# Softmax row sums by query halves, one reciprocal from PSUM, and a spread that is issued a pair later

## The chip, the cores and the metric

One core of a Trainium2 chip runs the kernel. The metric is the device time in microseconds of one execution. TensorE multiplies matrices, VectorE and ScalarE work on tiles (ScalarE has tanh, exp and silu), GpSimd here casts small tiles and issues transfers, SP issues the other transfers. Each engine takes its instructions in the order of the program; a waiting instruction holds up all that stand behind it on its engine.

## What is computed

```python
scores = scale * np.matmul(q, k.transpose(0, 1, 3, 2))      # 2 x 12 heads, 448 tokens, 64 wide
scores = cap * np.tanh(scores / cap)
attn = np.exp(scores - scores.max(-1)) / sum                 # softmax
x = attn @ v                                                 # 896 tokens x 768
h = x @ w_in;  g = h * sigmoid(1.702 * h);  x = g @ w_out     # 768 -> 2048 -> 768
xn = x / rms(x) * rms_g
out = (silu(xn @ w_gate) * (xn @ w_val)) @ w_out2            # 768 -> 1536 -> 768
```

All in float32. Matmuls whose operands are split into a high and a low part (float32r) take three products; the products with the exponentials as moving operand are plain float32, which TensorE runs as two passes, so one `matmul` call is two MATMUL instructions in the trace.

## The kernel before, in words

The program is written out in order by hand (a manual schedule), so the order of the calls is the order on every engine. It has two stages.

**Attention** (`attention`, L176 to L483) goes over 12 pairs of heads (NPR = 12). For pair p: `turn` transposes q and k (seven transposes), `split_kq` splits them on VectorE and casts a small block on GpSimd (L268); `scores(p, c)` for c = 0, 1, 2 makes the transposed scores of 128 keys by 448 queries for both heads, `scores_last` those of the last 64 keys of both heads in one tile; `exps` runs tanh and exp on ScalarE; the results are `pt[p, c]`, with keys on partitions. No maximum is subtracted. `outputs(p)` multiplies them with v into one PSUM bank, 64 partitions per head, and copies the bank to `zt[p]` (L331, for the last pair on ScalarE, L333). `sums(p)` multiplies them with ones to get the row sums.

The row sums have to reach all 64 partitions of a head, as reciprocals. For the first nine pairs `sums` makes two partial sums per head on 32 columns of the array each (L347: four products side by side, two rounds), copies the bank to SBUF (L352), and four small transfers on GpSimd's queue (L357) lay the 2 x 2 rows out over 128 partitions by 7. `recips(p)` adds the halves (L377), takes the reciprocal of 128 x 7 (L378) and sends it to DRAM (L380, the tile recs); `spread(p)` reads it back, each row to 64 partitions (L387, the tile r). For the last three pairs `sums` makes the sums on all 64 partitions of a head at once (L363, L368) and takes a reciprocal of 128 x 448 from PSUM (L373). `normal(p)` is `norm_mul` (L390, z times r), `norm_hi` (L395 or, for the last two pairs, L397 on ScalarE) and `norm_lo` (L401): it writes the high and low part of x.

The loop at L438 runs p = 0 to 12. In iteration p, in this order: exps(p, 0) and (p, 1); scores(p, 2); scores(p+1, 0); one decode operation; exps(p, 2); scores_last(p); turn and split of pair p+2; exps(p, 3); recips and spread of p-3; outputs(p-1); scores(p+1, 1); normal(p-4), and in the last two iterations normal(p-2) too; more decode operations; sums(p-1); loads. PSUM holds two tiles of scores, one of the turn (`ps_t`) and two banks (`ps_v`) that scores_last, outputs and sums share.

**Decode.** The weights arrive as 64-bit words; `square`, `sign`, `mask` and `high_part` on ScalarE and `mid`, `top`, `low` and `low_part` on VectorE turn a unit of them into a high and a low float32r part. `low(w)` also issues the load of unit w+3 on SP's queue (L151). The first four units are decoded within attention from a list of 30 operations (`early`, L417), of which each iteration from p = 3 on takes some in order.

**Feed-forward** (`rest`, L485 on) is three products per block (L541 to L543) and the last projection (L744). Its first six columns are units 0 to 2 on the first 384 tokens, then on the other 512; between the first and the second column `normal` of the last pair is issued (L605).

Of the kernel before, what the change touches and what calls it, by code (L numbers as in the profile page):

```python
# [18 lines left out]
def attn_moe_kernel(  # L19
# [38 lines left out]
    ones = keep.tile([128, 128], F32R, name="ones")  # L58
    gcol = keep.tile([128, KD], F32, name="gcol")
# [116 lines left out]
    def attention():  # L176
        with ExitStack() as actx:
# [19 lines left out]
            def constants():  # L197
# [5 lines left out]
                for e in range(2):  # L203
                    nc.gpsimd.memset(blk[half[e], half[e]], 1.0)
                    nc.gpsimd.memset(blk[half[e], half[1 - e]], 0.0)

# [127 lines left out]

            def sums(p):

                ps = ps_v.tile([128, 512], F32, tag="v", name="v")
                if p < NPR - 3:
                    for n in range(2):
                        for e in range(2):  # L340
                            for j in range(2):
                                if n and j:
                                    w, t = blk[:, 64 * e:64 * e + 32], pt[p, NC]
                                else:
                                    w, t = f(ones)[:, 0:32], pt[p, j + 2 * n][:, e]
                                r0 = 64 * e + 32 * j
                                nc.tensor.matmul(  # L347
                                    out=ps[r0:r0 + 32, 0:S], lhsT=w, rhs=t,
                                    start=(n == 0), stop=(n == 1), skip_group_check=True,
                                )  # L350
                    sc = zrp.tile([128, S], F32, tag="sc", name="sc", bufs=2)
                    nc.vector.tensor_copy(sc, ps[:, 0:S])  # L352
                    nr[p] = zrp.tile([128, 2, S // 64], F32, tag="rs", name="rs", bufs=3)
                    for e in range(2):
                        for j in range(2):
                            r0 = 64 * e + 32 * j
                            nc.gpsimd.dma_start(  # L357
                                out=nr[p][half[e], j], in_=sc[r0:r0 + 1, :].rearrange("o (a n) -> o a n", a=64)
                            )
                else:  # L360
                    for c in range(NC):
                        for e in range(2):
                            nc.tensor.matmul(  # L363
                                out=ps[half[e], 0:S], lhsT=f(ones)[:, half[e]], rhs=pt[p, c][:, e],
                                start=(c == 0), stop=False, skip_group_check=True,
                            )
                    for e in range(2):
                        nc.tensor.matmul(  # L368
                            out=ps[half[e], 0:S], lhsT=blk[:, half[e]], rhs=pt[p, NC],
                            start=False, stop=True, skip_group_check=True,  # L370
                        )
                    nr[p] = zrp.tile([128, S], F32, tag="r", name="r", bufs=3)
                    nc.vector.reciprocal(out=nr[p], in_=ps[:, 0:S])  # L373

            def recips(p):
                rs = nr[p]
                nc.vector.tensor_tensor(out=rs[:, 0], in0=rs[:, 0], in1=rs[:, 1], op=ALU.add)  # L377
                nc.vector.reciprocal(out=rs[:, 0], in_=rs[:, 0])  # L378
                nr[p] = dram.tile([2, S], F32, tag="recs", name="recs")
                nc.gpsimd.dma_start(  # L380
# [43 lines left out]
            def decode(n):  # L424
                for _ in range(min(n, len(early))):
                    run(*early.popleft())
# [423 lines left out]
```

## Time and profile before

| what | value |
|---|---|
| median of 3 runs (lowest to highest) | 639.77 us (637.91 to 642.45) |
| the profiled execution | 638.68 us |
| its span, first to last instruction | 636.9 us |
| TensorE busy | 612.9 us, 96% |
| VectorE busy | 437.8 us, 69% |
| ScalarE busy | 399.8 us, 63% |
| GpSimd busy | 82.8 us, 13% |
| mean granted TensorE clock | 0.994 |

Times in rows are microseconds from the start of the span. PE is TensorE, PEld its weight loads, DVE VectorE, ACT ScalarE, POOL GpSimd. A busy TensorE is one with a matmul in flight, not one at its peak. A row of the timeline gives start, duration, engine, line, operation, output and inputs with their shapes, and in brackets the idle time before it and what ended that. The granted clock is a share of 2.4 GHz.

### The profile page before, as it was taken

How to read it: one execution, taken by the hardware profiler on the slowest of the kernel's cores; microseconds unless marked ns; L12 is line 12 of the kernel's file. 1: busy time of each engine (PE TensorE's matmuls, PEld its weight loads, DVE VectorE, ACT ScalarE, POOL GpSimd, SP SyncE). 2: the span in 40 equal slices, each digit the busy share in tenths (PEclk: the TensorE clock that was granted, in tenths of full speed). 3: DMA queues.
4: the chain of work that ended last, by engine and by line, in shares of the span. 5: the costliest groups of instructions: out<-in, count | busy, mean ns of one | idle time of the engine just before them, and what ended most of it. 6: DMA issues, size and time to landing. Idle time of an engine off the chain costs nothing.

```text
span 636.9 us, 8389 instructions
## 1 busy us (share of the span) xinstructions
PE 612.9 (96%) x3251; PEld 511.6 (80%) x3251; DVE 437.8 (69%) x553; ACT 399.8 (63%) x533; POOL 82.8 (13%) x125
## 2 busy tenths in 40 slices
PE   7999878789999999999999999999999999999997
PEld 4544434348888998999888888999998899999997
DVE  2446765596768544566778889999378887588842
ACT  5999848719777564677867666668345676355500
POOL 2233432200000000000002220310012200023100
PEclk9999997999999999999999999999999999999999
DMA  5674523222334343133333423334323234143012
GB/s 132 151 187 118 132 52 97 78 65 81 118 103 146 104 145 99 51 100 125 125 99 100 143 64 102 139 100 150 98 69 131 99 100 150 58 134 106 0 57 117
DMA packets 86230, 67.22 MB, mean 106 GB/s; under 512 B 40228, under 2 KB 83510, under 8 KB 86192
## 3 DMA queue, kind: packets, MB, share of 16 engines
q1 hardware_dynamic: 80448, 64.27, 33.2%
q0 software_dynamic: 4784, 2.20, 1.4%
q8 instruction: 25, 0.41, 0.3%
q10 hardware_dynamic: 960, 0.23, 0.2%
q14 instruction: 13, 0.11, 0.1%
HBM read 63.80 MB, written 2.78 MB: 105 GB/s over the span
## 4 chain that ended last, share of the span: by engine, by line
PE 82%; DMA 8%; DVE 4%; ACT 3%; SPq 2%; issue 1%; POOL 0%; ACTq 0%; DVEq 0%; POOLq 0%
PE b L543 21%; PE b L542 21%; PE b L541 21%; PE b L744 14%; DMA r<-recs 4%; DMA recs<-rs 2%; PE v L320 2%; ACT tt L310 1%; PE s L288 1%; DMA kq<-in_q 1%; DVE r L373 1%; SPq L218 1%; DMA kq<-in_k 1%; DMA raw<-in_moe_w_in 1%; PE v L298 1%
## 5 line engine op out<-in xcount | busy, mean ns | idle before, releaser
L541 PE MATMUL b<-x,ring 128*128 128x512 f32 (+1 forms) x480 | 173.9, 362 | 2.0 <-DVE r L373 2.0
L543 PE MATMUL b<-x,ring 128*128 128x512 f32 (+1 forms) x480 | 174.2, 363 | 0.0
L542 PE MATMUL b<-x,ring 128*128 128x512 f32 (+1 forms) x480 | 174.0, 363 | 0.0
L541 PEld LDWEIGHTS b<-x,ring 128*128 128x128 f32 x480 | 90.1, 188 | 12.7 <-DVE r L373 2.3
L542 PEld LDWEIGHTS b<-x,ring 128*128 128x128 f32 x480 | 90.1, 188 | 9.8
L543 PEld LDWEIGHTS b<-x,ring 128*128 128x128 f32 x480 | 90.1, 188 | 9.4
L136 DVE SCALAR_TENSOR_TENSOR dec<-raw,dec 128x768 uint32<-128x768 uint32 x68 | 69.7, 1025 | 26.7 <-ACT dec L132 25.3
L744 PE MATMUL b<-ring,uA 128*128 128x384 f32 x504 | 87.8, 334 | 0.0
L744 PEld LDWEIGHTS b<-ring,uA 128*128 128x128 f32 x504 | 87.4, 188 | 0.0
L157 ACT ACTIVATE ring<-dec 128x768 fp32r<-128x768 f32 x68 | 56.7, 834 | 30.7 <-DVE dec L148 23.0
L142 DVE SCALAR_TENSOR_TENSOR dec<-raw,dec 128x768 uint32<-128x768 uint32 x68 | 73.2, 1076 | 1.1
L543 PE MATMUL b<-g,ring 128*128 128x384 f32 (+1 forms) x192 | 70.0, 365 | 0.0
L542 PE MATMUL b<-g,ring 128*128 128x384 f32 (+1 forms) x192 | 69.9, 364 | 0.0
L541 PE MATMUL b<-g,ring 128*128 128x384 f32 (+1 forms) x192 | 69.6, 362 | 0.0
L162 DVE TENSOR_TENSOR ring<-dec,ring 128x768 fp32r<-128x768 f32 x68 | 66.8, 984 | 3.6 <-ACT ring L157 3.6
L148 DVE SCALAR_TENSOR_TENSOR dec<-raw,dec 128x768 uint32<-128x768 uint32 x68 | 64.9, 955 | 1.4
L128 ACT ACTIVATE dec<-dec,edge 128x768 f32<-128x768 f32 x68 | 63.3, 932 | 0.9
L124 ACT ACTIVATE dec<-raw 128x768 f32<-128x768 f32 x68 | 61.0, 896 | 1.3 <-DVE ring L162 0.5
L132 ACT ACTIVATE dec<-dec 128x768 f32<-128x768 f32 x68 | 57.3, 843 | 1.5
L712 POOL TENSOR_TENSOR a<-a,gg 128x512 f32<-128x512 f32 (+1 forms) x18 | 29.7, 1648 | 188.6 <-DVE gg L705 188.6
L715 ACT ACTIVATE uA<-a 128x512 fp32r<-128x512 f32 (+1 forms) x24 | 13.9, 578 | 46.4 <-POOL a L712 34.5
L636 POOL TENSOR_TENSOR sqs<-sqs,sq 128x384 f32<-128x384 f32 (+1 forms) x10 | 11.7, 1169 | 236.0 <-ACT sq L632 236.0
(99 smaller groups left out, 706.9 us busy)
## 6 DMA issues: line engine op xcount, KB each, us to landing
raw<-in_moe_w_out SPq DMA_DIRECT2D x20, 768.0 KB, 4.2
raw<-in_moe_w_in SPq DMA_DIRECT2D x16, 768.0 KB, 4.6
raw<-in_moe_w_gate SPq DMA_DIRECT2D x12, 768.0 KB, 4.2
raw<-in_moe_w_val SPq DMA_DIRECT2D x12, 768.0 KB, 4.2
raw<-in_moe_w_out SPq DMA_DIRECT2D x8, 512.0 KB, 3.9
out<-oacc SPq DMA_DIRECT2D x6, 384.0 KB, 2.3
raw<-in_moe_w_out SPq DMA_DIRECT2D x8, 256.0 KB, 3.3
r<-recs POOLq DMA_DIRECT2D x9, 224.0 KB, 8.2
```

What stands on the lines that cost most here:

```text
L124: nc.scalar.activation(out=f(d), in_=f(r[:, :, 1]), func=AF.Square, scale=2.0 ** 15)
L128: nc.scalar.activation(out=f(d), in_=f(d), func=AF.Sign, bias=edge)
L132: nc.scalar.activation(out=f(d), in_=f(d), func=AF.Relu, scale=2.0 - 2.0 ** -23)
L136: nc.vector.scalar_tensor_tensor(out=d, in0=hi, scalar=3, in1=d, op0=ALU.logical_shift_left, op1=ALU.bitwise_and)
L142: nc.vector.scalar_tensor_tensor(out=d, in0=hi, scalar=0xC0000000, in1=d, op0=ALU.bitwise_and, op1=ALU.bitwise_or)
L148: nc.vector.scalar_tensor_tensor(out=d, in0=lo, scalar=29, in1=d, op0=ALU.logical_shift_right, op1=ALU.bitwise_or)
L157: nc.scalar.activation(out=t[:, 0], in_=f(dec_t[w][0]), func=AF.Copy)
L162: nc.vector.tensor_tensor(out=t[:, 1], in0=f(d), in1=f(t[:, 0]), op=ALU.subtract)
L541: nc.tensor.matmul(out=wide(o, b), lhsT=w0, rhs=x0, start=first, stop=False)
L542: nc.tensor.matmul(out=wide(o, b), lhsT=w0, rhs=x1, start=False, stop=False)
L543: nc.tensor.matmul(out=wide(o, b), lhsT=w1, rhs=x0, start=False, stop=last)
L744: nc.tensor.matmul(out=os_[t][n][:, 0:HW], lhsT=uA[xi][:, i, tok], rhs=w[:, wi, n * HW:(n + 1) * HW], start=(i == 0 and xi == 0 and wi == ...
```

## The change

- `sums` is one form for all pairs: for each head and each half of the 448 queries (224 columns), a product with ones (or, for the last keys, with `blk`) on 32 columns of the array, over all four blocks of keys. The result is 4 groups of 32 equal rows by 224 columns. One reciprocal of 128 x 224 reads it from PSUM.
- For the first nine pairs `keep_recips` sends one row of each group to DRAM right after `sums`; `spread` reads it back in the next iteration, ahead of that iteration's `sums`. The four small transfers, the copy, the add and `recips` are gone.
- For the last three pairs `spread_product` spreads the rows with four products with a selecting matrix `sel` (made by GpSimd at the start) into PSUM: pairs 9 and 10 in one tile of `ps_t` in iterations 11 and 12, pair 11 behind the first column of feed-forward. `norm_mul` reads them there.
- `norm_mul` writes into z in place of r; `norm_hi` of pair 10 is on VectorE.
- The decode list becomes a plan by iteration; what it has for p = 12 comes after the loop.

```diff
             def sums(p):
                 ps = ps_v.tile([128, 512], F32, tag="v", name="v")
...
+                for c in range(NC + 1):
                     for e in range(2):
                         for j in range(2):
+                            if c == NC:
+                                w, t = blk[:, 64 * e:64 * e + 32], pt[p, NC]
+                            else:
+                                w, t = f(ones)[:, 0:32], pt[p, c][:, e]
                             r0 = 64 * e + 32 * j
+                            nc.tensor.matmul(
+                                out=ps[r0:r0 + 32, 0:SH], lhsT=w, rhs=t[:, j * SH:(j + 1) * SH],
+                                start=(c == 0), stop=(c == NC), skip_group_check=True,
                             )
+                nr[p] = zrp.tile([128, SH], F32, tag="rs", name="rs", bufs=4)
+                nc.vector.reciprocal(out=nr[p], in_=ps[:, 0:SH])
+
+            def keep_recips(p):
+                rs = nr[p]
+                nr[p] = dram.tile([4, SH], F32, tag="recs", name="recs", bufs=3)
+                nc.gpsimd.dma_start(out=nr[p], in_=rs[0:128:32])
+
+            def spread(p):
+                d = nr[p].rearrange("(e j) n -> e (j n)", j=2)
+                nr[p] = zrp.tile([128, S], F32, tag="r", name="r", bufs=3)
+                nc.gpsimd.dma_start(out=nr[p], in_=d.unsqueeze(1).to_broadcast([2, 64, S]))
+
+            def spread_product(p, ps):
+                for j in range(2):
                     for e in range(2):
                         nc.tensor.matmul(
+                            out=ps[half[e], j * SH:(j + 1) * SH], lhsT=sel[:, 2 * e + j], rhs=nr[p],
+                            start=True, stop=True, skip_group_check=True,
                         )
+                nr[p] = ps[:, 0:S]
...
-            early = deque(
...
+            plan = {
+                3: [(square, 0), (sign, 0)], 4: [(mask, 0)], 5: [(square, 1), (mid, 0)],
+                6: [(sign, 1), (mask, 1), (top, 0), (low, 0)], 7: [(high_part, 0), (mid, 1)],
+                8: [(square, 2), (top, 1), (low_part, 0)], 9: [(sign, 2), (low, 1)],
+                10: [(mask, 2), (high_part, 1), (mid, 2)],
+                11: [(square, 3), (sign, 3), (top, 2), (low, 2), (low_part, 1)],
+                12: [(mask, 3), (high_part, 2), (low_part, 2), (mid, 3), (top, 3), (low, 3)],
+            }
...
-                if 3 <= p < NPR:
-                    recips(p - 3)
-                    spread(p - 3)
                 if p >= 1:
                     outputs(p - 1)
...
                 if p >= 4:
                     normal(p - 4)
+                if p == NPR - 1:
+                    late = ps_t.tile([128, 2, 512], F32, tag="t", name="late")
                 if p >= NPR - 1:
+                    spread_product(p - 2, late[:, p - NPR + 1])
                     normal(p - 2)
-                if 2 < p < NPR:
-                    decode((2, 3, 4)[max(0, p - NPR + 3)])
+                if p < NPR:
+                    decode(p)
+                if p >= 2 and p - 2 < NPR - 3:
+                    spread(p - 2)
                 if p >= 1:
                     sums(p - 1)
+                    if p - 1 < NPR - 3:
+                        keep_recips(p - 1)
...
+                        later(lambda: spread_product(q3, bank()))
                         later(*[lambda fn=fn: fn(q3) for fn in (norm_mul, norm_hi, norm_lo)])
```

## Rows read from the trace of the kernel before

**Rows 1.** The page's chain that ended last, by line

```profile
PE b L543 21%; PE b L542 21%; PE b L541 21%; PE b L744 14%; DMA r<-recs 4%; DMA recs<-rs 2%; PE v L320 2%; ACT tt L310 1%; PE s L288 1%; DMA kq<-in_q 1%; DVE r L373 1%; SPq L218 1%; DMA kq<-in_k 1%; DMA raw<-in_moe_w_in 1%; PE v L298 1%
```

**Rows 2.** Table of stretches: busy time (instructions) of each engine, granted clock

```profile
core 0: us, PE busy (x) PEld busy (x) DVE busy (x) ACT busy (x) POOL busy (x), PEclk, DMA share, GB/s
...
85.00:95.00 10.00, 6.71 (x47) 2.70 (x45) 6.61 (x12) 2.41 (x4) 4.22 (x9) 1.00 0.11 26
95.00:105.00 10.00, 6.70 (x28) 4.45 (x30) 3.31 (x5) 8.84 (x11) 2.70 (x5) 0.66 0.54 141
...
160.00:636.90 476.90, 473.54 (x2422) 434.21 (x2420) 346.25 (x421) 282.55 (x394) 41.35 (x28) 1.00 0.32 104
```

**Rows 3.** Timeline of VectorE, ScalarE and TensorE around 95 us

```profile
93.41 0.63 DVE L390 TENSOR_TENSOR r<-z,r 128x448 f32<-128x448 f32 x1 [2.30 <-DMA r<-recs]
...
96.03 0.84 ACT L157 ACTIVATE ring<-dec 128x768 fp32r<-128x768 f32 x1 [8.55 <-DVE dec L148]
...
97.82 1.49 PE L288 MATMUL s<-x 64*128 64x448 f32 x6 [4.96 <-ACT tt L310]
```

**Rows 4.** Waits in 14 to 143 us: total, times, longest

```profile
POOL r L387 <- DMA recs<-rs: 33.5, 9, 5.0
```

**Rows 5.** Timeline of VectorE: z copies of pairs 2 and 10

```profile
42.81 0.62 DVE L331 COPY z<-v 128x448 f32<-128x448 f32 x1 [0.60 <-PE v L325]
...
125.74 0.62 DVE L331 COPY z<-v 128x448 f32<-128x448 f32 x1 [3.56 <-PE v L325]
```

**Rows 6.** Timeline of TensorE: sums of pair 1 and iteration 3

```profile
34.87 1.31 PE L347 MATMUL v<-tt,ones 128*32 128x448 f32 x9
...
36.51 1.50 PE L288 MATMUL s<-x 64*128 64x448 f32 x12
...
39.51 2.48 PE L320 MATMUL v<-tt,vn 128*64 128x448 f32 x12
...
42.67 0.88 PE L288 MATMUL s<-x 64*128 64x448 f32 x6
43.47 1.31 PE L347 MATMUL v<-tt,ones 128*32 128x448 f32 x9
```

**Rows 7.** Groups by line and form, 0 to 143 us: busy, mean ns

```profile
L311 ACT ACTIVATE tt<-tt,capt 128x896 f32<-128x896 f32 x36 | 37.5, 1043 | 1.2
L310 ACT ACTIVATE tt<-s,tsc 128x896 f32<-128x896 f32 x36 | 35.8, 994 | 4.9 <-PE s L288 4.9
...
L373 DVE RECIPROCAL r<-v 128x448 f32<-128x448 f32 x3 | 8.9, 2954 | 0.0
...
L311 ACT ACTIVATE tl<-tl,capt 128x448 f32<-128x448 f32 x12 | 8.0, 669 | 0.4
...
L310 ACT ACTIVATE tl<-v,tsc 128x448 f32<-128x448 f32 x12 | 7.4, 617 | 0.0
...
L378 DVE RECIPROCAL rs<-rs 128x7 f32<-128x7 f32 x9 | 1.8, 201 | 0.3
```

**Rows 8.** Timeline of weight loads and matmuls within sums of pair 0

```profile
27.06 0.11 PEld L347 LDWEIGHTS v<-tt,ones 128*32 128x32 f32 x1 [0.25 <-issue]
27.07 0.54 PE L347 MATMUL v<-tl,blk 128*32 128x448 f32 x1
...
27.43 0.54 PE L347 MATMUL v<-tt,ones 128*32 128x448 f32 x1
```

**Rows 9.** Timeline of VectorE and TensorE at the end of attention

```profile
129.53 0.95 DVE L162 TENSOR_TENSOR ring<-dec,ring 128x768 fp32r<-128x768 f32 x1
...
133.25 2.95 DVE L373 RECIPROCAL r<-v 128x448 f32<-128x448 f32 x1
...
139.49 2.95 DVE L373 RECIPROCAL r<-v 128x448 f32<-128x448 f32 x1
...
137.14 0.45 PE L541 MATMUL b<-x,ring 128*128 128x384 f32 x1
...
142.49 0.44 PE L541 MATMUL b<-x,ring 128*128 128x384 f32 x1 [1.96 <-DVE r L373]
```

**Rows 10.** The tile recs: time to landing of both its transfers

```profile
DMA to landing us min/median/max: 1.7/6.0/9.0
```

More of the change, by code (lines that the diff above doesn't have):

```diff
@@ L58, in attn_moe_kernel @@
     ones = keep.tile([128, 128], F32R, name="ones")
+    sel = keep.tile([128, 4, 64], F32, name="sel")
     gcol = keep.tile([128, KD], F32, name="gcol")
@@ L205, in constants @@
                     nc.gpsimd.memset(blk[half[e], half[1 - e]], 0.0)
+                nc.gpsimd.memset(sel, 0.0)
+                for n in range(4):
+                    nc.gpsimd.memset(sel[32 * n:32 * n + 1, n], 1.0)
             xs, pt, zt, nr = {}, {}, {}, {}
@@ L333, in outputs @@
                     nc.scalar.activation(out=zt[p], in_=ps[:, 0:S], func=AF.Copy)
+            SH = S // 2
             def sums(p):
                 ps = ps_v.tile([128, 512], F32, tag="v", name="v")
[L338 to L353, printed above, removed]
+                for c in range(NC + 1):
@@ L367, in sums @@
+            def spread_product(p, ps):
+                for j in range(2):
                     for e in range(2):
                         nc.tensor.matmul(
-                            out=ps[half[e], 0:S], lhsT=blk[:, half[e]], rhs=pt[p, NC],
-                            start=False, stop=True, skip_group_check=True,
-                        )
[L372 to L380, printed above, removed]
-                    out=nr[p].rearrange("e s -> (e s)").rearrange("(p n) -> p n", p=128), in_=rs[:, 0]
-                )
@@ L384, in spread @@
[L384 to L387 removed]
+                            out=ps[half[e], j * SH:(j + 1) * SH], lhsT=sel[:, 2 * e + j], rhs=nr[p],
+                            start=True, stop=True, skip_group_check=True,
+                        )
+                nr[p] = ps[:, 0:S]
             def norm_mul(p):
[L390 removed]
+                nc.vector.tensor_tensor(out=zt[p], in0=zt[p], in1=nr.pop(p), op=ALU.mult)
@@ L399, in norm_lo @@
             def norm_lo(p):
                 b, pp = divmod(p, NP)
-                nc.vector.tensor_tensor(out=xA[1][:, pp, b * S:(b + 1) * S], in0=nr.pop(p), in1=f(xA[0][:, pp, b * S:(b + 1) * S]), op=ALU.subtract)
+                xx = slice(b * S, (b + 1) * S)
+                nc.vector.tensor_tensor(
+                    out=xA[1][:, pp, xx], in0=zt.pop(p), in1=f(xA[0][:, pp, xx]), op=ALU.subtract
+                )
             nc.vector.memset(f(xA[0][:, 0, 0:S]), 1.0)
@@ L415, in attention, with decode @@
                 nc.tensor.matmul(out=warm[:, 0:S], lhsT=ones, rhs=xA[0][:, 0, 0:S], start=True, stop=True)
-            early = deque(
-                [(square, 0), (sign, 0), (mask, 0), (square, 1), (mid, 0), (sign, 1), (top, 0), (mask, 1), (low, 0)]
-                + [(high_part, 0), (mid, 1), (square, 2), (low_part, 0), (sign, 2), (top, 1), (mask, 2), (low, 1)]
-                + [(high_part, 1), (mid, 2), (square, 3), (low_part, 1), (top, 2), (sign, 3), (low, 2)]
-                + [(high_part, 2), (mask, 3), (low_part, 2), (mid, 3), (top, 3), (low, 3)]
-            )
-            def decode(n):
-                for _ in range(min(n, len(early))):
-                    run(*early.popleft())
+            plan = {
[6 more added lines that the diff above has]
+            }
+            def decode(p, n=9):
+                for _ in range(min(n, len(plan.get(p, ())))):
+                    run(*plan[p].pop(0))
             def normal(p):
@@ L448, in attention @@
                         s0 = scores(p + 1, 0)
-                    if p > 2:
-                        decode(1)
+                    decode(p, 1)
                     exps(p, 2, s2)
@@ L481, in attention, with rest @@
                     load_to((1, 2, 4).index(p))
-            decode(len(early))
-            return norm_mul, norm_hi, norm_lo
-    def rest(norm_mul, norm_hi, norm_lo):
+            decode(NPR)
+            return spread_product, norm_mul, norm_hi, norm_lo
+    def rest(spread_product, norm_mul, norm_hi, norm_lo):
         with ExitStack() as fctx:
```

20 lines of the change are left out of this document (3 added, 17 removed).

## The prediction

> **What bounds the kernel now.** I read the chain that ended last first [rows 1]. It is mostly the feed-forward matmuls L541 to L543 and L744, but 6% of it (by these rounded shares up to 38 us) is two tiny transfers, recs<-rs and r<-recs: the spreading of the softmax sums. Next I read the table of stretches [rows 2]: from 160 us on TensorE is busy 473.5 of 476.9 us, so that part is full and ends when it begins plus a constant. Between 85 and 105 us TensorE is busy two thirds of the time and ScalarE 2.4 of the first 10 us, and the granted clock of the second ten is 0.66, that is, it ran part of it at 1.2 instead of 2.4 GHz after the idle time. So the gain is to be had in attention (0 to 142 us).
>
> The timeline shows why it idles [rows 3]: VectorE stands 2.30 us at normal's L390 for r<-recs; behind it in its order is a decode operation (L148) for which ScalarE's L157 stood 8.55 us, and behind L157 in ScalarE's order is the tanh for which TensorE stood 4.96 us. The cause stands on GpSimd's queue: in each iteration L387 waits there for the landing of L380's transfer, 33.5 us in nine waits [rows 4], because `recips`, `spread` and the four small transfers of `sums` share one in-order queue, and `normal` wants the result one iteration later.
>
> Where nothing stalls, TensorE sets the pace: in the iteration of p=3 no row but the last matmuls' own succession is seen, sums at 34.87, two scores, the last scores and the turn from 36.51, outputs from 39.51, scores from 42.67, sums again at 43.47 [rows 6]. That is 1.64 + 3.00 + 3.16 + 0.80 = 8.60 us a pair. ScalarE needs, for a pair, (37.5 + 35.8 + 8.0 + 7.4) / 12 = 7.39 us [rows 7] and some 12 decode operations of 0.84 [rows 3] over nine iterations, 1.1 each: 8.5. It is just under TensorE, which I keep in mind below.
>
> **The change part by part.**
>
> *The hop.* Per pair four issues (rs<-sc), the copy, the add and the small reciprocal go; one reciprocal of 128x224, one transfer out and one spread stay. The spread of pair p is now issued in iteration p+2, when its recs transfer has been under way for most of an iteration, and `normal` takes it in p+4. From the first issue (about 10 us into iteration p+1) to `normal` (about 7 into p+4) there are some 3 x 8.6 - 3 = 22.6 us. The two transfers took 1.7 to 9.0 us to land, median 6.0 [rows 10]; even two of the longest, 18 us, and the 1.4 us of issuing fit. So I cost the hop at nothing; its cover is these 22.6 us, and beyond them VectorE would stand at L390 again, one for one. What is late next is TensorE's own succession.
>
> *Sums on TensorE, first nine pairs.* Before: 8 products in two passes, 16 matmuls of 448 columns, four side by side: one four starts at 27.07, the next at 27.43, 0.37 us [rows 8], and the block takes 1.64 [rows 6]. After: 32 matmuls of 224 columns, eight fours. At half the columns a four takes 0.19, so 8 x 0.19 + 0.1 for the change of shape = 1.6: no difference. Bounds: the four weight loads take 0.11 each at once [rows 8]; if they were not covered by the four that is running, 8 x 0.11 = 0.9 more. Below, nothing can be gained but the 0.1. I take 0, since the load at 27.06 runs beside a four that ends at 27.43 [rows 8], and 0.19 still covers 0.11.
> The Trainium skill ("TensorE: Matmul & The Clock Gate", Part 3, The mechanism) speaks against this: it says that a weight load overlaps with running matmuls only where the row group differs, and all of these use all 128 rows. By that rule the sum would be 0.9 us more per pair. The trace does not bear it out at 448 columns: the load starts while matmuls on the same rows run.
>
> *Sums, last three.* The 64-column form pairs two, so 16 matmuls were 8 x 0.37 = 3.0 us; now 1.6. Added is the spread by products: 4 products in two passes, two side by side, 224 columns: 4 x 0.19 + 0.1 = 0.9. Bounds: 0.8 and, with loads of twice as many columns (up to 0.22) uncovered in each of the four steps, 1.7. Net 0.5 us less each.
>
> *Reciprocals.* 128x448 took 2.954 us and 128x7 took 0.201 [rows 7]: 6.24 ns a column, so 224 columns take 0.20 + 217 x 0.00624 = 1.55. For the last three that is 1.4 less. For the first nine it replaces the copy (0.62 as the z copies of the same shape [rows 5]), the small one (0.20) and an add, under 1.0 together: 0.6 us more of VectorE per pair, which stood idle between its waits even so. But it holds the PSUM bank 0.9 longer. The next to want a bank is the following outputs, 3.0 us (the second stretch of rows 6) after the sums end. VectorE reaches the reciprocal in time when its z copy and normal (0.62 + 1.6) and at most one decode operation lie between, ending 1.6 to 2.5 after the sums; with two (iterations 6 and 8) 0.1 to 0.2 late. Cost 0 to 0.3 in all.
>
> *The decode plan* moves operations among iterations 3 to 12, at most two extra per iteration on ScalarE; four VectorE operations (low_part of unit 2; mid, top, low of unit 3) come behind the last reciprocal, where they lie beside two feed-forward columns. GpSimd's five new memsets fall in its idle time ahead of the first casts. `low` also issues a weight load on SP's queue, and SP waits there until `low` is done: for units 0 and 1 this moves from iterations 5 and 8 to 6 and 9, so that behind it stand only the v loads of iteration 6, wanted in iteration 9. GpSimd otherwise waits for recs behind the casts and for the reciprocal; only its own next casts stand behind, for scores an iteration away.
>
> **The sum.** Both kernels do the same up to the z copy of pair 2 at 42.81; that of pair 10 was at 125.74 [rows 5], 82.9 us later. After: six full iterations. TensorE alone gives 8.60; I take 8.75, since ScalarE's 8.5 alternates with iterations of one or two decode operations: 52.5. Iteration 10 has no turn: 7.8. Iteration 11 has neither turn nor next scores: up to its outputs 0.80 + 1.64 + 1.6 + 3.16 = 7.2. Sum 67.5, so z of pair 10 at 110.3: 15.4 us earlier.
>
> From that z to the second feed-forward column: before 142.49 - 125.74 = 16.75 [rows 5, 9]. After, VectorE: z and two normals 129.53 - 125.74 = 3.8, three decode operations of (133.25 - 129.53) / 4 = 0.93 each 2.8, reciprocal of pair 10 1.5: 8.1. TensorE has by then done the spread of pair 9 (0.9), sums 10 (1.6) and outputs 11 (3.2), 5.7, and waits 2.4 us for that reciprocal with the spread of pair 10 (0.9); sums 11 (1.6) end at 10.6, the first column (142.49 - 1.96 - 137.14 = 3.4 with its fill, 3.2 in succession) at 13.8, and spread 11 (0.9) at 14.7. Reciprocal 11 starts when normal 10 is through, 8.1 + 0.9 + 1.6 = 10.6, and ends at 12.2, hidden by that column, which is why the wait of 1.96 at L541 [rows 9] goes. Gain 16.75 - 14.7 = 2.1.
>
> Together 17.5 us. What follows L541 at 142.49 is full TensorE time and I leave it as it is. The profiled execution took 638.68 us (span 636.9 and 1.8 around it): 638.7 - 17.5 = 621.2. The median of the runs is 1.1 above the profiled one, within their own spread, so I say 621.5.
>
> **The rivals.**
> *Short matmuls pay for their loads.* For: the cover shrinks from 0.37 to 0.19 while the load stays at 0.11. Against: it still fits. 0.9 us in each of the iterations 4 to 12: 8 us of the gain go, about 629.5. The rule named above ends here.
> *Given back at the start of feed-forward.* The low operation that releases a weight buffer to the next load lies 9 us ahead of the second column now (the decode that ends at 133.25 [rows 9]) and about 2 us behind it after; ScalarE's decode may then wait for the weights and TensorE for the decode. Against: the first six columns (some 20 us) use units decoded before. 1 to 5 us; about 624 to 626, with other friction between ScalarE and TensorE (9.2 instead of 8.75 an iteration, 2.7 us) in the same place.
> *No gain:* the stalls stay, since spread or its landing is late after all; 638.
> *Slower: the reciprocal closes a ring.* VectorE stands at L390 for r, then reaches the next reciprocal late, and that now holds the PSUM bank and starts the next hop: lateness beyond the 1.4 us between the reciprocal's end and the next outputs goes to TensorE every iteration. It decides against the change when a hop takes over 22.6 + 1.4 = 24 us, against 1.7 to 9.0 twice; with 28 us nine iterations lose 4 each, 36 less the 17.5 gained: 657, and from 26 us on it is slower than before.
>
> **How the numbers follow.** Forecast 0.76 (its own range 617 to 626); loads uncovered 0.09; given back more than that 0.08; no gain 0.04; ring 0.03. Lower end: iterations at 8.6 save 0.9, and without the 2.4 us wait at the spread of pair 10, and with ScalarE's pace never met, 615. Upper end takes in the loads: 631. About 1% is what a measurement tells from no change: faster than 633.4 in 0.93, within in 0.04, slower in 0.03.
>
> **What would show it.** z copies 8.6 to 8.9 apart between 43 and 95 us, and no wait of VectorE for r at `norm_mul`; GpSimd's wait of 33.5 us nearly gone; the clock at 1.00 in every stretch; eight fours 0.19 apart in sums; reciprocals of 1.55; a wait of some 2.4 us ahead of the spread of pair 10; the second column at 124 to 126. Wrong if fours stand 0.3 apart, if VectorE stands for r, if the z copies are over 9.2 apart, or if TensorE idles after 125 us.

## The result, and the profile after

The changed kernel takes 623.64 us, the median of 4 runs (623.58 to 624.70); the kernel before took 640.09 beside it (4 runs, 637.91 to 642.45). The ratio is 0.9746, 95% interval 0.9710 to 0.9783: faster by about 2.5%. The forecast was 621.5 with a range of 615 to 631 and a chance of 0.93 for faster; the time lies 2.1 us above the forecast and within its own range of 617 to 626. The profiled execution took 623.68 us with a span of 621.9.

The chain that ended last, by line, answers to [rows 1]:

```profile
PE b L540 22%; PE b L539 22%; PE b L538 22%; PE b L742 14%; PE v L324 4%; PE s L292 3%; PE v L352 2%; PE v L329 1%; PE v L302 1%; DMA kq<-in_q 1%; DVE rs L357 1%; PE t L250 1%; DVE z L379 0%; DVE dec L143 0%; DVE z L335 0%
```

No transfer of the softmax sums is left on it; the one load that is left is that of q at the start. The table of stretches, with the columns of [rows 2], has two stretches more, for the clock:

```profile
core 0: us, PE busy (x) PEld busy (x) DVE busy (x) ACT busy (x) POOL busy (x), PEclk, DMA share, GB/s
17.00:21.00 4.00, 3.27 (x26) 2.40 (x27) 2.18 (x2) 3.93 (x5) 0.58 (x2) 1.00 0.44 100
85.00:95.00 10.00, 9.87 (x86) 5.10 (x82) 7.93 (x10) 9.59 (x11) 2.52 (x6) 1.00 0.32 78
95.00:105.00 10.00, 9.98 (x104) 5.37 (x107) 6.45 (x10) 9.13 (x12) 1.36 (x2) 1.00 0.37 106
...
120.00:124.00 4.00, 4.00 (x38) 2.42 (x37) 3.08 (x5) 0.00 (x0) 0.00 (x0) 0.57 0.16 57
160.00:621.90 461.90, 458.53 (x2348) 420.69 (x2346) 334.64 (x407) 270.47 (x376) 41.35 (x28) 1.00 0.32 104
```

Between 85 and 105 us TensorE is now busy 19.85 of 20 us, at a granted clock of 1.00, where before it was busy 13.4 and partly at 1.2 GHz. From 160 us on nothing is new. What is new is the stretch from 120 to 124 at 0.57: TensorE is busy all of it, but mostly at 1.2 GHz.

VectorE's timeline, for [rows 5]:

```profile
42.90 0.62 DVE L335 COPY z<-v 128x448 f32<-128x448 f32 x1 [0.91 <-PE v L329]
...
51.50 0.62 DVE L335 COPY z<-v 128x448 f32<-128x448 f32 x1 [0.91 <-PE v L329]
52.04 0.62 DVE L379 TENSOR_TENSOR z<-z,r 128x448 f32<-128x448 f32 x1
...
53.96 1.56 DVE L357 RECIPROCAL rs<-v 128x224 f32<-128x224 f32 x1 [0.22 <-PE v L352]
...
110.93 0.62 DVE L335 COPY z<-v 128x448 f32<-128x448 f32 x1 [3.35 <-PE v L329]
...
117.44 1.55 DVE L357 RECIPROCAL rs<-v 128x224 f32<-128x224 f32 x1
```

The z copies of pairs 2 and 3 stand 8.60 us apart, and `norm_mul` (L379) follows its copy at once: no wait for r, here or in any other iteration. TensorE's timeline, for [rows 6, 9]:

```profile
34.95 1.34 PE L352 MATMUL v<-tt,ones 128*32 128x224 f32 x24
36.12 0.56 PE L352 MATMUL v<-tl,blk 128*32 128x224 f32 x8
36.61 1.49 PE L292 MATMUL s<-x 64*128 64x448 f32 x12
...
107.63 2.48 PE L324 MATMUL v<-tt,vn 128*64 128x448 f32 x12 [0.63 <-DVE rs L357]
...
119.05 0.98 PE L372 MATMUL late<-rs,sel 128*64 128x224 f32 x8 [2.63 <-DVE rs L357]
119.96 2.28 PE L352 MATMUL v<-tt,ones 128*32 128x224 f32 x24
...
122.91 0.69 PE L538 MATMUL b<-x,ring 128*128 128x384 f32 x1
...
127.48 0.44 PE L538 MATMUL b<-x,ring 128*128 128x384 f32 x1
```

The sums of a pair take 36.61 - 34.95 = 1.66 us, as before. The last sums, after the wait of 2.63 us, take 122.91 - 119.96 = 2.95 for the same work: that is the low clock. The second feed-forward column starts at 127.48.

Three points of the timelines divide the span: the z copy of pair 2, that of pair 10, and the start of the second feed-forward column. "Body" is the stretch between the first two, "tail" that to the third, "rest" all behind it. All are from single profiled executions, in us.

| kernel | z of pair 2 | z of pair 10 | second column | span | body | tail |
|---|---|---|---|---|---|---|
| before | 42.81 | 125.74 | 142.49 | 636.9 | 82.93 | 16.75 |
| after | 42.90 | 110.93 | 127.48 | 621.9 | 68.03 | 16.55 |
| before, later use | 44.34 | 120.16 | 138.53 | 634.5 | 75.82 | 18.37 |
| before, new plan | 43.00 | 123.05 | 138.81 | 634.7 | 80.05 | 15.76 |
| before, both | 44.12 | 116.93 | 136.29 | 632.0 | 72.81 | 19.36 |
| after, old list | 43.10 | 119.95 | 138.51 | 632.9 | 76.85 | 18.56 |
| after, earlier use | 44.51 | 114.25 | 131.64 | 626.0 | 69.74 | 17.39 |
| after, old last three | 44.72 | 115.08 | 130.66 | 626.5 | 70.36 | 15.58 |
| after, filled | 44.50 | 112.51 | 127.44 | 621.8 | 68.01 | 14.93 |
| after, again | 44.65 | 112.68 | 127.59 | 622.0 | 68.03 | 14.91 |
| after, filled again | 42.99 | 111.00 | 125.92 | 620.3 | 68.01 | 14.92 |
| after, recs first | 44.24 | 112.24 | 128.50 | 622.9 | 68.00 | 16.26 |
| after, decode last | 44.29 | 112.30 | 124.49 | 618.9 | 68.01 | 12.19 |
| after, reciprocal first | 44.50 | 111.76 | 123.94 | 618.3 | 67.26 | 12.18 |

Of the 15.0 us between the two spans, the body gave 14.9 (forecast 15.4), the tail 0.2 (forecast 2.1), and the rest is 494.4 in both. The medians are 16.5 apart, 1.5 more than the spans: the profiled execution of the kernel before, 638.68 us, is one of its quicker ones.

### The profile page after: what moved, and what is told of

It reads as the page before. It is cut to its first block, busy times and chain, and to the rows that moved or that the text cites. A ratio compares the mean times of both kernels' runs of the same rounds, so it can differ in the third digit from the quotient of the medians.

```text
span 621.9 us, 8747 instructions
## 1 busy us (share of the span) xinstructions
PE 609.1 (98%) x3467; PEld 516.8 (83%) x3467; DVE 439.9 (71%) x536; ACT 398.6 (64%) x532; POOL 65.1 (10%) x94
## 4 chain that ended last, share of the span: by engine, by line
PE 93%; DVE 4%; DMA 1%; SPq 1%; issue 1%; ACT 0%; ACTq 0%; DVEq 0%
PE b L540 22%; PE b L539 22%; PE b L538 22%; PE b L742 14%; PE v L324 4%; PE s L292 3%; PE v L352 2%; PE v L329 1%; PE v L302 1%; DMA kq<-in_q 1%; DVE rs L357 1%; PE t L250 1%; DVE z L379 0%; DVE dec L143 0%; DVE z L335 0%
## 5 line engine op out<-in xcount | busy, mean ns | idle before, releaser
L570 DVE TENSOR_TENSOR g<-gg,g 128x384 fp32r<-128x384 f32 (+1 forms) x32 | 20.0, 626 | 31.6 <-ACT g L567 31.4
```

## The experiments

### What the stall was made of, from the kernel before

My theory was that the gain is the hop's: whoever lets the spread sums come in time has the gain. The simplest test takes the normalisation a pair later in the kernel before and leaves everything else.

```diff
-                if p >= 4:
-                    normal(p - 4)
+                if p >= 5:
+                    normal(p - 5)
+                if p == NPR:
+                    normal(p - 4)
```

(The tiles z and r get a buffer more each.)

> The kernel before, with nothing changed but that the result of the hop is used one iteration later: normal(p-5) in place of normal(p-4), with one more buffer for z and r; the last iteration has one normal more on VectorE (1.6 us). Theory A, that the gain is the slack between the spread's issue and its use: r lands about 11 us after recips, which is 3 us too late for normal now and 5 us early then, so VectorE no longer stands at L390, TensorE runs at 8.6 to 8.9 us a pair, the z copy of pair 10 comes at 111 to 114 us and the time is 624 to 629 us. Rival B, that the four small transfers and the recips on the shared queue had to go: GpSimd stays the bound, the z copies stay 9.5 or more apart, 634 to 640 us.

Measured: 634.46 us (634.26 to 636.28), ratio 0.9893 (0.9847 to 0.9939), 6.0 less than the 640.47 beside it. The rival's number held, though not its reason, as the rows show. The timelines of ScalarE and VectorE in this run:

```profile
90.67 0.84 ACT L157 ACTIVATE ring<-dec 128x768 fp32r<-128x768 f32 x1 [5.04 <-DVE dec L148]
...
87.43 0.62 DVE L331 COPY z<-v 128x448 f32<-128x448 f32 x1 [0.60 <-PE v L325]
87.97 0.61 DVE L390 TENSOR_TENSOR r<-z,r 128x448 f32<-128x448 f32 x1
...
89.59 1.04 DVE L148 SCALAR_TENSOR_TENSOR dec<-raw,dec 128x768 uint32<-128x768 uint32 x1
...
102.10 0.62 DVE L331 COPY z<-v 128x448 f32<-128x448 f32 x1 [0.64 <-PE v L325]
```

VectorE no longer stands for r: L390 runs right behind the copy. Up to pair 7 the copies are 8.6 to 8.7 apart, not the 9.5 of a GpSimd that bounds them. But then one iteration takes 102.10 - 87.43 = 14.67, and ScalarE still stands 5.04 us for L148. The old list puts `low(1)` and, right behind it, `high_part(1)` into the same decode slot of iteration 8. VectorE can reach `low(1)` only behind the z copy and the three operations of `normal`; ScalarE is by then long through with its tanh and exp, and `high_part(1)` keeps it from those of the next pair. The stall had a second cause, which [rows 3] had shown: ScalarE stood 8.55 us there while VectorE stood 2.30, so some 6.2 of it could not come from that wait.

The other half alone, the new decode plan in the kernel before, and then the two together:

```diff
-            early = deque(
...
+            plan = {
+                3: [(square, 0), (sign, 0)], 4: [(mask, 0)], 5: [(square, 1), (mid, 0)],
...
-                    if p > 2:
-                        decode(1)
+                    decode(p, 1)
...
-                if 2 < p < NPR:
-                    decode((2, 3, 4)[max(0, p - NPR + 3)])
+                if p < NPR:
+                    decode(p)
```

> The kernel before with nothing changed but the decode plan of the changed kernel (operations by iteration, the last six behind the loop). Theory D, that there were two causes side by side, the hop that comes late and the old list's high_part right behind the low of the same unit, for which ScalarE stood 5.0 us in iteration 8 even where the hop was early: without the list the iteration of 16.7 us goes to about 10 and that of 10.7 to 9, but the waits for r stay, so the z copies stay 9 to 10 apart: 8 to 10 us less than before, 630 to 633 us. Rival A (the slack alone): the long iteration was the hop's, the plan brings 0 to 3 us, 637 to 640.

Measured: 637.83 us (10 runs, 635.02 to 640.41), ratio 0.9942 (0.9916 to 0.9968), 2.9 less than 640.74. Two rows of VectorE's timeline tell why it is so little:

```profile
65.04 0.63 DVE L390 TENSOR_TENSOR r<-z,r 128x448 f32<-128x448 f32 x1 [4.23 <-DMA r<-recs]
...
94.41 0.63 DVE L390 TENSOR_TENSOR r<-z,r 128x448 f32<-128x448 f32 x1 [3.22 <-DMA r<-recs]
```

The waits for r stay: the wait of the second row was 2.30 in [rows 3], the first was 2.69 in the kernel before, and between 14 and 143 us they are 16.2 us in seven, 13.4 in six before. From the z copy of pair 7 to that of pair 8 it is now 11.19 us instead of 16.72. But from pair 9 to pair 10 it is 13.16 instead of 10.74: there VectorE stands 2.04 for r with the long reciprocal behind it, the outputs wait 2.62 for that, and TensorE goes on at the low clock (0.57 from 118 to 122).

> The kernel before with both the result of the hop used one iteration later (normal(p-5)) and the new decode plan, but with its old sums, its four small transfers, recips, and its old last three pairs. Theory D: both causes are gone, z copies 8.6 to 8.9 apart up to pair 8, and nearly the whole gain is there without the new sums: 624 to 628 us (one normal more in the last iteration, 1.6). Rival: the whole reciprocals and fewer transfers carry part of the gain, 630 us or more.

Measured: 633.69 us (632.50 to 633.96), ratio 0.9873 (0.9828 to 0.9919), 7.05 less than 640.74; the rival's side again. In the body the two parts add up: 7.1 and 2.9 alone, 10.1 together. What is left of the changed kernel's 14.9 is something else. With both stalls gone the z copies are 8.6 apart up to pair 7 and 8.8 to the next, and then a third wait comes. The timelines of VectorE, TensorE and GpSimd:

```profile
105.69 0.17 DVE L377 TENSOR_TENSOR rs<-rs 128x7 f32<-128x7 f32 x1 [6.20 <-DMA rs<-sc]
...
112.06 4.04 PE L320 MATMUL v<-tt,vn 128*64 128x448 f32 x12 [3.07 <-DVE r L373]
...
67.10 0.83 POOL L387 DMA_DIRECT2D r<-recs  x1 [5.30 <-DMA recs<-rs]
...
86.33 0.83 POOL L387 DMA_DIRECT2D r<-recs  x1 [6.71 <-DMA recs<-rs]
87.16 2.12 POOL L357 DMA_DIRECT2D rs<-sc  x4
...
106.03 0.83 POOL L387 DMA_DIRECT2D r<-recs  x1 [5.61 <-DMA recs<-rs]
```

GpSimd issues one spread at 67.10 and the last at 106.03, four pairs later: 9.7 us a pair against 8.6 of TensorE. A pair costs its queue the wait for recs (44.7 us in nine), the four issues of `sums` (2.1), the casts (0.65) and two issues more (0.57 and 0.83): about 9.1 in all. So the old hop's queue falls behind at full pace, and the small transfers behind it come late: VectorE stands 6.20 for them, and the reciprocal of 2.95 us behind that holds up the outputs, which then take 4.04 us for their twelve matmuls instead of 2.48, at a granted clock of 0.59 (112 to 116 us).

### The same parts, from the kernel after

The old order of decode in the new kernel (the plan filled with the old list's operations, iteration by iteration):

```diff
-                3: [(square, 0), (sign, 0)], 4: [(mask, 0)], 5: [(square, 1), (mid, 0)],
...
+                3: [(square, 0), (sign, 0), (mask, 0)], 4: [(square, 1), (mid, 0), (sign, 1)],
...
+                7: [(low_part, 0), (sign, 2), (top, 1)], 8: [(mask, 2), (low, 1), (high_part, 1)],
...
```

> The changed kernel with the decode operations in the old order, three to five per iteration from the fourth on, instead of the new plan. Theory: the new plan matters little within the body, since the stalls were those of the hop; three operations per iteration give ScalarE up to 9.4 us in some iterations and VectorE two or three before the reciprocal, so iterations of 8.7 to 9.2 us, 2 to 4 us more by the end, and one VectorE operation more ahead of the reciprocal of pair 10 (0.9) but four fewer behind: 625 to 628 us. Rival: the plan is a main part of the gain (ScalarE's long waits were for decode operations): 632 us or more.

Measured: 633.49 us (632.12 to 636.14), ratio 0.9872 (0.9811 to 0.9934), 9.9 more than the changed kernel. The body is 8.8 longer, in two iterations, 14.15 for pair 8 and 11.43 for pair 10: those in which the old list has `low` and `high_part` of one unit side by side. The timelines of ScalarE and TensorE at the first:

```profile
89.60 0.84 ACT L158 ACTIVATE ring<-dec 128x768 fp32r<-128x768 f32 x1 [4.96 <-DVE dec L149]
...
91.39 0.87 PE L292 MATMUL s<-x 64*128 64x448 f32 x6 [2.54 <-ACT tt L314]
```

The new hop is in, VectorE waits for no r, and ScalarE stands 4.96 us all the same.

The normalisation a pair earlier, to measure how much slack the hop has:

```diff
-                if p >= 4:
-                    normal(p - 4)
+                if 3 <= p < NPR:
+                    normal(p - 3)
```

> The changed kernel with normal(p-3) in place of normal(p-4): the result of the hop is used one iteration earlier, all else as it is. In its trace the spread of pair p-2 goes out about 11 us after the start of iteration p and takes some 8 to land, about 5 us ahead of normal. Theory A (slack): one iteration less makes it 3 to 4 us late, VectorE stands at norm_mul in most iterations, and since the next reciprocal, which feeds the next hop and frees a PSUM bank, stands behind it, TensorE loses 1 to 4 us in each of eight iterations: 632 to 655 us, which is most of the gain gone or the slower ring. Rival B (fewer transfers, shorter hop): the hop is short enough in any case, 623 to 626 us.

Measured: 630.93 us (627.83 to 631.19), ratio 0.9821 (0.9771 to 0.9870), 7.3 more than the changed kernel, between the two theories. VectorE now waits for r in five iterations, 0.38 to 0.98 us each, as here:

```profile
81.32 0.63 DVE L379 TENSOR_TENSOR z<-z,r 128x448 f32<-128x448 f32 x1 [0.96 <-DMA r<-recs]
...
115.85 0.63 DVE L379 TENSOR_TENSOR z<-z,r 128x448 f32<-128x448 f32 x1 [0.98 <-DMA r<-recs]
```

So the slack is under one iteration of 8.6 us. (The profiled execution is the quickest of the four, 627.83. Its body is 1.7 us longer and its tail 2.5 longer than 14.91; where the others lose 3 us more was not seen.)

The last three pairs in the old way (64 columns, reciprocal of 448 columns, no product):

```diff
             def sums(p):
...
+                if p >= NPR - 3:
...
+                    nc.vector.reciprocal(out=nr[p], in_=ps[:, 0:S])
+                    return
...
-                    spread_product(p - 2, late[:, p - NPR + 1])
```

> The changed kernel with the last three pairs as before (sums on 64 columns, reciprocals of 448 columns, no spread by products). My sum before the change gave 2 to 3 us for this part; the kernel with both other causes removed lost about 3.0 us in the step from pair 9 to 10, where outputs waited 3.07 us for a reciprocal of 2.95, and 2.8 us in the tail. Theory E, that the last three's form is a third cause: 628 to 631 us. Rival: it brings nothing, as the tail of 16.55 us against 16.75 suggests, 623 to 625.

Measured: 626.53 us (624.99 to 628.27), ratio 0.9773 (0.9740 to 0.9805), 3.0 more than the unchanged kernel beside it (623.50), between the two. The timelines of VectorE and TensorE, against the wait of 0.63 at 107.63 above:

```profile
108.77 2.96 DVE L357 RECIPROCAL r<-v 128x448 f32<-128x448 f32 x1 [0.85 <-PE v L352]
...
111.78 2.48 PE L324 MATMUL v<-tt,vn 128*64 128x448 f32 x12 [1.45 <-DVE r L357]
```

The long reciprocal holds the bank that the outputs want.

### The order on GpSimd's queue

In the changed kernel the profile showed a wait that the prediction had said would go; the same row before is in [rows 4]:

```profile
POOL r L367 <- DMA recs<-rs: 39.1, 8, 7.7
```

It grew from 33.5 to 39.1 us. The transfer recs, 3.5 KB, is issued right behind the spread of the pair before, 224 KB on the same queue. The experiment swaps them:

```diff
-                if p >= 2 and p - 2 < NPR - 3:
-                    spread(p - 2)
                 if p >= 1:
                     sums(p - 1)
                     if p - 1 < NPR - 3:
                         keep_recips(p - 1)
+                if p >= 2 and p - 2 < NPR - 3:
+                    spread(p - 2)
```

> The changed kernel with the transfer to DRAM of pair p-1 issued ahead of the spread of pair p-2 instead of behind it, on the same queue. Theory: the small transfer takes 7.3 us to land (4.1 before) because it stands behind the spread's 224 KB; ahead of it, it lands in 2 to 4, GpSimd's waits for recs fall from 39.1 to under 12 us, and since nobody waits for r, the time stays: 623 to 625 us. Rival: the landing is long because only four partitions are read, then it stays at 7, and so does the wait or its like.

Measured: 623.73 us (621.97 to 624.69), ratio 0.9712 (0.9658 to 0.9766): the same time. The waits of GpSimd and the transfers (size, median us to landing) of this kernel:

```profile
POOL recs L362 <- DVE rs L357: 44.9, 9, 6.0
...
POOL r L367 <- DMA recs<-rs: 2.0, 1, 2.0
```

```profile
recs<-rs POOLq DMA_DIRECT2D x9, 3.5 KB, 3.0
```

and the transfers of the changed kernel:

```profile
r<-recs POOLq DMA_DIRECT2D x9, 224.0 KB, 8.5
...
recs<-rs POOLq DMA_DIRECT2D x9, 3.5 KB, 7.3
```

Ahead of the spread recs lands in 3.0 us, behind it in 7.3. But now GpSimd waits for the reciprocal instead, 44.9 us. Nothing that bounds the time stands behind either wait.

### The tail

Why did the tail give 0.2 and not 2.1? The wait of 2.63 us ahead of the spread of pair 10 was forecast (2.4); the low clock behind it was not. Twelve matmuls on known data, written where the spread's product goes next, fill the wait:

```diff
                 if p >= NPR - 1:
+                    if p == NPR:
+                        for _ in range(12):
+                            nc.tensor.matmul(
+                                out=late[:, 1, 0:S], lhsT=ones, rhs=xA[0][:, 0, 0:S], start=True, stop=True
+                            )
                     spread_product(p - 2, late[:, p - NPR + 1])
```

> The changed kernel with 12 matmuls of no use (float32r, 448 columns, about 0.19 us each, 2.3 us in all) in the 2.63 us that TensorE waits for the reciprocal ahead of the spread of pair 10. The wait itself stays. Theory C, that the granted clock falls to 1.2 GHz after that idle time and that this makes the sums of pair 11 take 2.95 instead of 1.64 us and the first column 3.7 instead of 3.2: the clock stays at 1.00, the second column starts at 125.5 to 126 instead of 127.48, 621.8 to 622.2 us. Rival: the clock falls for another reason (the form of the matmuls, or the time that has run), then the time is 623.6 or up to 0.5 more.

Measured: 623.52 us (621.85 to 623.62), ratio 0.9710 (0.9665 to 0.9755): no gain in the median. Yet the tail is 14.93, 1.6 shorter. In this execution the low clock lay elsewhere: the z copy of pair 2 came at 44.50, 1.6 later than in the changed kernel. To see whether that was chance, the unchanged kernel and the filled one ran again side by side:

> The changed kernel once more, unchanged, beside the three that follow, for comparisons on the same chip. Theory: 623.5 to 625.5 us, depending on whether the clock falls in the first 7 us of an execution (that costs 1.4 us: the z copy of pair 2 at 44.3 instead of 42.9).

> The kernel with the 12 filling matmuls once more. Theory C (the clock falls after the 2.63 us of idle time and costs 1.6 us): 1.4 to 1.8 us less than a_again in the median of the same call, 621.8 to 623.9. Rival: the same time as a_again.

Measured: 623.50 (5 runs, 621.96 to 623.77, ratio 0.9717, 0.9689 to 0.9744) and 623.59 (5 runs, 622.10 to 623.67, ratio 0.9726, 0.9698 to 0.9755). The expected gain of the filling did not come. The unchanged kernel, run again, has another trace than the first time; TensorE's timeline and the stretches:

```profile
120.80 0.98 PE L372 MATMUL late<-rs,sel 128*64 128x224 f32 x8 [2.63 <-DVE rs L357]
121.71 1.34 PE L352 MATMUL v<-tt,ones 128*32 128x224 f32 x24
...
123.36 0.45 PE L538 MATMUL b<-x,ring 128*128 128x384 f32 x1
```

```profile
17.00:21.00 4.00, 4.00 (x21) 3.18 (x23) 1.70 (x2) 2.36 (x3) 0.46 (x2) 0.57 0.44 98
121.00:125.00 4.00, 4.00 (x49) 2.87 (x46) 3.86 (x7) 0.00 (x0) 0.00 (x0) 1.00 0.37 131
```

The same wait of 2.63 us, and no fall of the clock behind it: the sums take 123.36 - 121.71 = 1.65, and the tail is 14.91 (forecast 14.7). But the stretch from 17 to 21 us, at 1.00 the first time, is at 0.57, and everything from there on is 1.7 us later (0.6 of it was there already when the first scores of pair 1 start). The waits of TensorE just ahead are the same in both, 1.27 and 0.56 us. The low stretch lies from 17 to 21 us, not in the first 7 us, where the expectation put it.

Is it one low stretch in each execution, early or late? Two more traces say no. That of "recs first" (the order of GpSimd's queue turned, as above) has both, 0.57 from 17 to 21 us and 0.72 in the stretch with the wait and the sums:

```profile
17.00:21.00 4.00, 4.00 (x23) 3.06 (x19) 2.09 (x2) 2.75 (x3) 0.26 (x1) 0.57 0.44 101
...
119.00:125.00 6.00, 4.64 (x44) 2.63 (x45) 5.05 (x8) 0.79 (x2) 0.00 (x0) 0.72 0.43 131
```

"Filled again" has neither: 1.00 from 17 to 21 and 1.00 from 119 to 125. The early stretch comes and goes by itself. It costs 1.0 to 1.3 us (from the first scores of pair 1 to the z copy of pair 2, 28.7 to 29.0 us with it against 27.7 without); the late one costs 1.3 to 1.6 (tails of 16.26 and 16.55 against 14.91). The times of these executions go with them: 622.10 with neither, 623.62 to 623.77 with one, 624.69 with both. Of the unchanged kernel, two runs at a mean clock of 0.999 took 621.96 and 622.11, the three at 0.997 took 623.50 to 623.77. In the three traces with the wait unfilled the late stretch is low in two, in the two traces with it filled in none. That the filling keeps the clock up there is therefore possible, but not shown; in the medians nothing came of it.

The wait itself can go without filling. Ahead of the reciprocal it waits for, VectorE runs three decode operations; here they move behind it:

```diff
-                11: [(square, 3), (sign, 3), (top, 2), (low, 2), (low_part, 1)],
-                12: [(mask, 3), (high_part, 2), (low_part, 2), (mid, 3), (top, 3), (low, 3)],
+                11: [(square, 3), (sign, 3)],
+                12: [(low_part, 1), (top, 2), (low, 2), (mask, 3), (high_part, 2), (low_part, 2), (mid, 3), (top, 3),
+                     (low, 3)],
```

> The changed kernel with the three VectorE decode operations of iteration 11 (top and low of unit 2, low_part of unit 1) moved behind the reciprocal of pair 11. Theory: the reciprocal of pair 10 then ends about 2.8 us earlier, TensorE no longer waits 2.63 us for it, the clock stays at 1.00, and the second feed-forward column starts 12 to 13 us after the z copy of pair 10 instead of 16.55: 619 to 621 us. Rival: the first columns then wait for their weights (low_part of units 1 and 2 and the following loads come later), and half or all is given back: 622 to 624 us.

Measured: 619.38 us (619.22 to 620.67), ratio 0.9658 (0.9613 to 0.9703), 4.3 less than the changed kernel's 623.64. TensorE's timeline has no wait left there:

```profile
116.87 0.92 PE L329 MATMUL v<-tl,ve 128*64 128x448 f32 x4
117.69 0.98 PE L372 MATMUL late<-rs,sel 128*64 128x224 f32 x8
...
124.49 0.44 PE L539 MATMUL b<-x,ring 128*128 128x384 f32 x1
```

The tail is 12.19: 2.7 below the 14.91, the wait. Of the 4.3 us between the medians, the rest is the clock: three of its four runs are at 0.999 to 1.000 (619.22 to 619.48), where the changed kernel's four are all at 0.997. Runs of like clock differ by about 2.8, the wait: 619.22 to 619.48 against 621.96 and 622.11, and 620.67 against 623.50 to 623.77. That fewer low stretches come of the missing wait is not shown: in the next kernel, which has no wait there either, three of five runs are at 0.997 again, and the traces of both kernels have the early stretch. The rest behind the second column is not longer for the operations that it now has beside it (618.9 - 124.49 = 494.4).

The same on a smaller scale: in iterations 8 and 10 too, the reciprocal goes ahead of the decode operations.

```diff
-                if p < NPR:
+                if p < NPR and p not in (8, 10):
                     decode(p)
...
+                if p in (8, 10):
+                    decode(p)
```

> The kernel with the decode of iteration 11 moved behind the last reciprocal, and in iterations 8 and 10 the decode operations behind the sums and their reciprocal as well. Theory: the two waits of outputs for the reciprocal that stands behind a decode operation (0.63 us at pair 10, 0.2 at pair 8) go, 0.7 to 0.9 us less than the 619.4 of the kernel without this: 618.3 to 618.9, or 1.4 more with the fall of the clock at the start. Rival: nothing, as the turn's split on VectorE is then late.

Measured: 619.90 us (5 runs, 618.49 to 620.15), ratio 0.9661 (0.9634 to 0.9688). Its median is no better, but runs of like clock are: 618.49 at 0.999 against 619.22 to 619.48. The body is 67.26, 0.75 shorter, and the row that answers to 107.63 of the changed kernel has no wait:

```profile
107.51 0.88 PE L302 MATMUL v<-x,kb 128*128 128x448 f32 x3
108.46 2.48 PE L324 MATMUL v<-tt,vn 128*64 128x448 f32 x12
```

These last two are ahead of both kernels, by about 4 and 21 us in the medians.

## Why the prediction was right, and where its reasons were not

**The body.** Forecast 67.5, measured 68.03. The six full iterations took 8.60, 8.62, 8.60, 8.93, 8.62 and 8.81, 52.2 together against "six full iterations ... 52.5". The 8.93 (a wait of 0.26 for the reciprocal) and the 8.81 (8.60 with the order turned) are the iterations 6 and 8 that were said to come 0.1 to 0.2 late. "TensorE's own succession" is indeed what is late next. ScalarE's sum was a little low, since the plan has 13 operations for it in iterations 3 to 11 and not "some 12": 8.6 in place of 8.5, as much as TensorE needs, which none of these iterations shows as a loss. Iteration 10 took 7.91 (forecast 7.8). Iteration 11 took 7.94 against 7.2: the step that was mis-sized is the PSUM bank that the reciprocal holds, "cost 0 to 0.3 in all". There a decode operation stands ahead of the reciprocal while no next scores fill the time; the outputs wait 0.63, and with the order turned the iteration takes 7.39.

**Sums and reciprocals.** Held: 1.66 us for 32 matmuls, with eight fours in it, so 0.21 a four, and reciprocals of 1.55 to 1.56. The rival of uncovered loads did not come: with a load of 0.11 ahead of each four, 0.19 would have become 0.30. The Trainium skill ("TensorE: Matmul & The Clock Gate", Part 3, The mechanism) would, by its line on what overlaps, have a load of the same row group wait for the running matmuls; the trace disagrees at 224 columns (0.21 a four) as it did at 448 (0.37).

**The tail.** Forecast 14.7, measured 16.55 in the profiled execution and 14.91 in the second one. The working was right: the wait "of some 2.4 us" was 2.63, the spread by products 0.9, the second column came at 127.48 (124 to 126 was said) and at 127.59 with a start 1.7 later. The step that failed is "the clock at 1.00 in every stretch". Most executions have a low stretch, at one of two places or at both, of 1.0 to 1.6 us each. The two runs of the changed kernel at a mean clock of 0.999, 621.96 and 622.11, lie half a microsecond above the forecast of 621.5.

**Given back at the start of feed-forward.** Did not happen: the rest is 494.4 us in both kernels.

**What the gain was owed to.** Here the reasons were wrong though the sum was right. The prediction read [rows 3] as one stall with one cause, the hop, and gave the decode plan no term of its own: it "moves operations among iterations 3 to 12", with the weight buffers as the only thing weighed. The runs show that the hop alone (later use) is worth 6.0 us, the plan alone 2.9, both 7.05, and that the plan is worth 9.9 once everything else is in. The sum came out since it was not a sum of stalls removed, but TensorE's pace counted up anew; that form needs only that every cause is removed, and this change removed them all. A change with the new hop and the old list would have been forecast at the same 621.5 and come out at 633.5.

**The third part.** "Per pair four issues (rs<-sc), the copy, the add and the small reciprocal go": the hop was costed at nothing. It is more: the old queue of GpSimd takes about 9.1 us a pair at full pace, the new one 39.1 / 8 = 4.9 of waiting and 0.80, 0.57 and 0.65 of work, 6.9. It stays below 8.6. The new hop and the last three pairs together are the 10.05 us from 633.69 to 623.64; 3.0 of them are shown to be the last three's. That the queue set the pace is shown by the trace of "both"; how much of the other 7 is the queue's is not, for it was not tried alone. By the table 4.8 of them lie in the body, 2.3 of which the last three's old form brings back there, and 2.8 in the tail, where "both" also has one `normal` (1.6 us on VectorE) more. The writing of `norm_mul` into z and the move of `norm_hi` of pair 10 were not tried by themselves either.

**The slack.** "22.6 us" from the first issue to `normal` was near (3 x 8.6 - 3 is 22.8; measured 18.8 to 22.4), but little of it is slack. The spread is issued only 10.5 to 17.9 us before its use (108.37 and 118.91 for pair 8) and lands in 8.5 at the median: 2.0 to 9.4 us are left, 4 to 6 in most of the iterations. The prediction let recs go out right behind its reciprocal and land undisturbed; it lands in 7.3 us, behind the spread, and GpSimd waits for that before the next spread. "GpSimd's wait of 33.5 us nearly gone" failed for the same reason. The ring of the slower rival is nearer than it was said to be: with use one pair earlier it costs 7.3 us.

## What to carry to other kernels

When two engines stand idle one behind the other, compare the lengths of their waits: what the first engine's wait does not account for in the second's has a cause of its own. Where a stall has several causes, one that is undone in the slow kernel can show little, since a later wait takes back what it gave, and the same one put back in the fast kernel shows its worth (the decode plan: 2.9 and 9.9; for the use a pair later the two are nearly alike, 6.0 and 7.3); do both. And in an order written by hand, whatever releases a bank or feeds the busy engine goes ahead of work that nobody waits for yet: three decode operations moved behind a reciprocal took a wait of 2.6 us away, and about 2.8 us of the time between runs of like clock.

## What was not expected of the hardware

The granted clock after the same wait of 2.63 us, with the same instructions around it, fell in one execution (0.57 in the four microseconds from 120) and not in another (1.00). A second low stretch, from 17 to 21 us, came in some executions and not in others, with the late one and without it. They cost 1.3 to 1.6 and 1.0 to 1.3 us. What decides was not found.

A transfer of 3.5 KB took 7.3 us to land behind a spread of 224 KB on the same queue and 3.0 ahead of it, with the same number of issues.
